# Nine pinned w2^T blocks with ScalarE casts, an input-gradient pass by tiles, and two orders, in a fused spectral and MLP layer with its gradients

## The chip, the cores and the metric

The kernel runs on one core of a Trainium2 chip. The metric is the device time of one execution in microseconds (us); the kernel before took 1411.57 us, the median of 3 runs (1410.99 to 1412.05). Besides the engines of the profile (PE is TensorE, DVE VectorE, ACT ScalarE, POOL GpSimd, SP SyncE) the kernel uses PSUM tiles of 128 x 512 in three groups: two buffers of "s", two of "d" and four of "f".

## What is computed

A layer with adaptive layer norms, a spectral mixer and a channel MLP, with its output and the gradients of all nine inputs by which it depends on parameters or data. x is 2048 x 1024, the MLP is 1024 to 3584 and back, all in bf16.

```python
def A(x, w_r, w_i):                       # spectral mixer
    X = rfft2(x) * (w_r + 1j * w_i)
    return irfft2(X, s=(2048, 1024))
def B(x, w1, b1, w2, b2):                 # MLP
    h = gelu(layernorm(x) @ w1 + b1)
    return h @ w2 + b2
def f(A_x, A_w_r, A_w_i, w1, b1, w2, b2, c, w_mod):
    sa, ca, ga, sb, cb, gb = split6(silu(c) @ w_mod)
    x = A_x
    x = x + ga * A(layernorm(x) * (1 + ca) + sa, A_w_r, A_w_i)
    return x + gb * B(layernorm(x) * (1 + cb) + sb, w1, b1, w2, b2)
out, vjp = jax.vjp(f, ...); return out, *vjp(grad_out)
```

## The kernel before

The transforms are done as matmuls on folded data: even and odd halves are formed by additions on DVE ("fold"), multiplied with cosine and sine matrices on PE, and taken apart again ("unfold"). The stages stand in this order, and the work of several lies beside each other, since the tile framework orders each engine's queue ahead of time by priorities and dependencies. Every engine takes its own queue in order.

**Front.** The modulation rows come from pm matmuls (mod_block, line 278, and its evacuation in line 281). At the same time the product of w2 with the transposed gradient, called ph, is begun: 28 blocks of 128 rows of w2^T, each of four PSUM tiles of 8 matmuls of 128x512 (ph_part, pp in line 814), so 32 matmuls for a block. A tile is cast to bf16 (line 820) into phs, a ring of four blocks in SBUF (three in pho, one in phr), and a block is stored on the POOL queue (line 822). Its w2 rows come by a transposing DMA on SP into wt, also a ring of four (load_w2t, line 341; block n can be loaded once block n-4 has been multiplied). PH_EARLY (line 824) says how many blocks are pinned: here 6 in a loop that also loads the blocks to come and puts the later pm groups behind blocks 3 and 5, and one more behind it (line 834). The last of these matmuls is early_pe, and the first matmuls of the forward spectral part may only be issued after it (line 537). The other blocks (line 897) are free: the scheduler puts them wherever PE has room within the spectral part and after it, and loads blocks from PH_EARLY + 4 on there.

**Forward fold.** For four chunks of x, the statistics (DVE and ACT), the norm (norm_act, line 514, four ACT instructions for a chunk), the modulation (line 194, the helper that records all tensor_tensor operations) and the fold fill fbuf. The last addition (fold_in) also releases the memset of css, a pair of staging buffers.

**Forward spectral part.** s_fwd multiplies fbuf with smA or smB (pu, lines 531 and 538; the forward pu use only the two "s" buffers) and copies to U, pcs (line 577), the filter pairs, pv (line 647), po (line 749), then consume_fwd: unfold, the residual, the second layer norm, and a store of the normed chunk. The copies of pu, pcs and pv are left to the framework's choice of engine (act_copy, line 778).

**MLP forward and the gradient at its inside.** z_block multiplies with w1 (pz, line 951) and evaluates the gelu and its derivative on ACT (lines 954 to 964) and DVE; z0 comes first, then the last blocks of ph, then z1 and on; pbo (line 1005) is the second MLP product.

**Input gradient, in quarters b of 512 rows.** pg_pass (line 1099) multiplies the gradient inside the MLP with w1^T: for each half h of the 1024 columns, four PSUM tiles i (128 rows each) and seven groups g of four matmuls, g outer and i inner, 28 steps of four matmuls. All four tiles are complete only in the last group. They are evacuated on ACT (line 1121, with their row sums). In quarters after the first, DVE and ACT run the layer-norm gradient (ln_bwd: lines 1199 to 1204, where ACT's line 1203 waits for two small DVE results), and fold the quarter into fbuf. The strip sums (acc3a, line 217) of the quarter before are put behind chosen steps of pg_pass by "behind". At the end the backward spectral part starts with pu (line 538) from this fbuf.

**Backward spectral part and w1's gradient.** The backward spectral part is interleaved by hand with products of the w2 and w1 gradients: fill(n) issues n pieces, where a piece of w1's gradient is one tile of 16 matmuls (gw1acc, line 1464, evacuated to gwo in line 1468). In consume_bwd (line 1376 on) a chunk i is followed by fill((4, 7, 6, 8)[i]), then a sum on PE over the product ct (halves_sum, accCA in line 217), then fill(2). After the spectral part the gradient of sa is scaled by ACT into sr (line 1521), whose buffer px0 was that of xt, the chunk of x that DVE reads in consume_bwd. Then the rest of w1's gradient fills PE to the end.

Of the kernel before, what the change touches and what calls it, by code (L numbers as in the profile page):

```python
# [10 lines left out]
FP32 = mybir.dt.float32  # L11
# [6 lines left out]
P = 128  # L18
S = 2048
D = 1024  # L20
# [3 lines left out]
NFC = F // P  # L24
KH = D // 2
# [5 lines left out]
NB = 4  # L31
# [4 lines left out]
def kernel(  # L36
# [24 lines left out]
    nc = tc.nc  # L61
# [4 lines left out]
    reg = ctx.enter_context(tc.tile_pool(name="reg", bufs=1))  # L66
# [6 lines left out]
    def ps_s(name):  # L73
        return psum.tile([P, 512], FP32, tag="s", name=name)
# [4 lines left out]
    def ps_f(name):  # L79
        return psum.tile([P, 512], FP32, tag="f", name=name, bufs=4)  # L80
# [44 lines left out]
    def chunk_rows(dt, i):  # L125
        return dt[4 * i * P:4 * (i + 1) * P, :].rearrange("(q p) d -> p q d", p=P)
# [14 lines left out]
    def load_tok(t4, src, i, eng=None):  # L141
        s3 = tok_flat(src)
        ins = (eng or nc.sync).dma_start(out=tok_plain(t4, i), in_=tok_rows(s3, i, 0, D))  # L143
        for q in range(2):
            nc.gpsimd.indirect_dma_start(out=t4[:, tok_idx(i, q), :], out_offset=None, in_=s3,  # L145
                                         in_offset=bass.IndirectOffsetOnAxis(ap=xidx[:, 2 * i + q:2 * i + q + 1], axis=0))
        return ins
# [45 lines left out]
    def tt(out, a, b, op):  # L193
        return nc.vector.tensor_tensor(out=out, in0=a, in1=b, op=op)  # L194
# [121 lines left out]
    def unfold_d(o4, tmp):  # L316
        n = o4.shape[1]
        ov = o4.rearrange("p c (a b w) -> p c a b w", b=2, w=256)
        tv = tmp.rearrange("p c (s b w) -> p c s b w", s=2, w=256)
        tt(tv[:, :, 0], ov[:, :, :, 0, :], ov[:, :, :, 1, :], ALU.add)  # L320
        tt(tv[:, :, 1], ov[:, :, :, 0, :], ov[:, :, :, 1, :], ALU.subtract)
        fwd = o4.rearrange("p c (b w) -> p c b w", w=512)[:, :, :, 0:256]
        rev = bass.AP(tensor=o4.tensor, offset=o4.offset + 1023, ap=[o4.ap[0], [D, n], [-512, 2], [-1, 256]])
        tt(fwd, tv[:, :, :, 0, :], tv[:, :, :, 1, :], ALU.add)
        tt(rev, tv[:, :, :, 0, :], tv[:, :, :, 1, :], ALU.subtract)

    def unfold_tok(o4, tmp):
        tt(tmp[:, 0:4:2, :], o4[:, 0:4:2, :], o4[:, 1:4:2, :], ALU.add)
        tt(tmp[:, 1:4:2, :], o4[:, 0:4:2, :], o4[:, 1:4:2, :], ALU.subtract)
        tt(o4[:, 0:4:3, :], tmp[:, 0:2, :], tmp[:, 2:4, :], ALU.add)  # L330
        tt(o4[:, 1:3, :], tmp[:, 0:2, :], tmp[:, 2:4, :], ALU.subtract)
# [8 lines left out]
    def load_w2t(fc):  # L340
        w2t_in[0] = nc.sync.dma_start_transpose(out=wt[:, fc % 4], in_=B_w2[fc * P:(fc + 1) * P, :])
        w2ts.append(w2t_in[0])
# [40 lines left out]
    for j in range(4):  # L383
        for cch in range(NDC):
            pt = ps_f("pt")
            for a in range(4):
                q = (0, 2, 3, 1)[a] if j % 2 == 0 else (1, 3, 2, 0)[a]
                nc.tensor.matmul(pt[:, q * P:(q + 1) * P], lhsT=gos[j][:, a, cch * P:(cch + 1) * P], rhs=(ident, irev)[a // 2],
                                 start=True, stop=True)
# [129 lines left out]
    def behind(ins, later):  # L519
        tc.add_manual_dep(ins.ins, later.ins.name, mybir.DependencyInfo(mybir.DependencyClass.NoSync, mybir.DependencyReason.DATA),  # L520
                          reason="order")
# [282 lines left out]
    last_pe = [None]  # L804
# [4 lines left out]
    def ph_part(fc, js):  # L809
        ph2 = phs[fc % 4]  # L810
        for j in js:
            pp = ps_f("pp")
            for cch in range(NDC):
                last_pe[0] = nc.tensor.matmul(pp[:], lhsT=wt[:, fc % 4, cch, :], rhs=gBoT[j][:, cch, :],  # L814
                                              start=(cch == 0), stop=(cch == NDC - 1))
            q = (0, 2, 3, 1)[j]
            ov = ph2[:, :, q * P:(q + 1) * P]
            pv = pp[:, :].rearrange("p (i w) -> p i w", w=P)
            with tc.high_priority():
                nc.any.tensor_copy(out=ov, in_=pv)  # L820
        if js[-1] == 3:
            nc.gpsimd.dma_start(out=d_ph[fc * P:(fc + 1) * P, :], in_=ph2.rearrange("p i w -> p (i w)"))

    PH_EARLY = 6
    late_mods = [(r, h) for r in (2, 3, 4) for h in range(2)]
    for fc in range(PH_EARLY):
        ph_part(fc, (0, 1, 2, 3))
        load_w2t(fc + 4)
        if fc in (3, 5):
            with tc.issue_after(last_pe[0].ins):  # L830
                for r, h in late_mods[3 * (fc // 2 - 1):3 * (fc // 2)]:
                    mod_block(r, h)

    ph_part(PH_EARLY, (0, 1, 2, 3))
    early_pe = last_pe[0]

    for i in range(4):
# [50 lines left out]
    def load_w1(n):  # L888
        for _ in range(n):
            g = len(w1s)  # L890
            wtile = reg.tile([P, NDC, BW], BF16, name=f"w1_{g}", tag=W1T[g])
            with tc.issue_after(w2t_in[0].ins):
                w1_in.append(nc.sync.dma_start(out=wtile[:], in_=w1_v[:, :, g * BW:(g + 1) * BW]))
            w1s.append(wtile)

    PH_KEEP = NFC - 4
    for fc in range(PH_EARLY + 1, NFC):
        if fc >= PH_EARLY + 4:
            load_w2t(fc)
            load_w1({24: 1, 25: 1, 27: 5}.get(fc, 0))  # L900
        ph_part(fc, (0, 1, 2, 3) if fc < PH_KEEP else (0, 1))
# [165 lines left out]
    w1Ts = []  # L1067
    gzr = [reg.tile([P, 2, 4, BW], BF16, name=f"gzr{k}", tag=f"t{k}") for k in range(4)]
    gzs, g_sums, gn3s = {}, {}, {}

    def gn3_of(b):
        if b % 2 not in gn3s:
            gn3s[b % 2] = reg.tile([P, 4, D], BF16, name=f"gn3{'ab'[b % 2]}", tag=("uv3", "wt")[b % 2])
        return gn3s[b % 2]
# [11 lines left out]
    for g in range(7):  # L1086
        wtile = reg.tile([P, 4, D], BF16, name=f"w1T_{g}", tag=W1T[g])
        for k in range(4):
            fc = g * 4 + k
# [6 lines left out]
    last_pg = [None]  # L1096
    sums_in = [[], [], []]

    def pg_pass(b, h, pool, before=lambda: ExitStack()):
        pgs = [pool(k)("pg") for k in range(4)]  # L1100
        for g in range(7):
            for i in range(4):
                for k in range(4):
                    with before():
                        last_pg[0] = nc.tensor.matmul(pgs[i][:], lhsT=gzs[b, g][:, k, i * P:(i + 1) * P],  # L1105
                                                      rhs=w1Ts[g][:, k, h * KH:(h + 1) * KH],
                                                      start=(g == 0 and k == 0), stop=(g == 6 and k == 3))
                    last_pe[0] = last_pg[0]
                g0 = 3 if b == NB - 1 else 2
                if b > 0 and h == 0 and (g, i) in ((g0, 0), (g0 + 1, 2), (g0 + 2, 2)):  # L1110
                    for ins in sums_in[g - g0]:
                        behind(ins, last_pg[0])
                    sums_in[g - g0].clear()
            for k in range(4 if b < 2 and h == 1 else 0):
                nc.scalar.activation(out=gzs[b, g][:, k, :], in_=gzs[b, g][:, k, :], func=ACT.Identity,
                                     accum_out=gb1_acc[:, g * 4 + k, b:b + 1])
            if g < 6:
                yield
        for i in range(4):
            with tc.high_priority():  # L1120
                nc.scalar.activation(out=gn3_of(b)[:, i, h * KH:(h + 1) * KH], in_=pgs[i][:], func=ACT.Identity,  # L1121
                                     accum_out=g_sums[b][:, h, i:i + 1])
        yield
# [248 lines left out]
    def consume_bwd(i, o4, tmp, tmp2, n1, eb):  # L1372
        if i == 0:
            accCA.append(ps_s("accCA"))
            nc.vector.tensor_copy(out=sacc, in_=eb[:, 0, :])
        elif i == 2:
            tt(sacc, sacc, eb[:, 0, :], ALU.add)
        unfold_d(o4, tmp)
        unfold_tok(o4, tmp)
        load_tok(n1, A_x, i, nc.gpsimd)  # L1380
        with tc.issue_after(last_po[0].ins):
            norm_act(n1, n1, 0, i)
        tt(tmp, o4, n1, ALU.mult)
        s1c = small.tile([P, 4], FP32, tag="s1c")
        for q in range(4):
            t = 4 * i + q
            nc.vector.tensor_tensor_reduce(out=o4[:, q, :], in0=o4[:, q, :], in1=opca_row, scale=1.0, scalar=0.0,  # L1387
                                           op0=ALU.mult, op1=ALU.add, accum_out=s1c[:, q:q + 1])
            ln_bwd(o4[:, q, :], s1c[:, q:q + 1], n1[:, q, :], stats[:, 0, 0, t:t + 1], o4[:, q, :], tmp2[:, q, :])
        nc.sync.dma_start(out=n1, in_=chunk_rows(d_gx1, i))  # L1390
        tt(o4, o4, n1, ALU.add)
        store_tok(out_1, o4, i)
        fill((4, 7, 6, 8)[i])
        halves_sum(accCA[0], tmp, i == 0, i == 3)
        fill(2)
        if i == 3:
            rows = small.tile([P, D], BF16, tag="gmrow", bufs=1)
            store_halves(accCA[0], rows[0:64, 0:KH], tmp, 1)
# [77 lines left out]
    def fill(n):  # L1476
        for _ in range(n):
            next(todo)
        done[0] += n
# [36 lines left out]

    accSA = [ps_d("accSA0"), ps_d("accSA1")]
    colsum(accSA, sacc, True, True)
    sr = reg.tile([P, 2, 1, D], FP32, name="sr", tag="px0")
    for h in range(2):  # L1520
        nc.scalar.mul(out=sr[0:1, 0, 0, h * KH:(h + 1) * KH], in_=accSA[h][0:1, :], mul=8.0)
    unfold_d(sr[0:1, 0], sr[0:1, 1])
# [48 lines left out]
```

## Time and profile before

| | |
|---|---|
| time, median of 3 runs | 1411.57 us (1410.99 to 1412.05) |
| time of the profiled execution | 1412.42 us |
| its span, first to last instruction | 1410.6 us |
| mean granted clock of PE | 0.992 |
| busy: PE, DVE, ACT, POOL | 1374.2, 1072.4, 739.2, 351.2 us |
| matmuls | 6963 |

Rows of a timeline give the start, the time that the group takes, engine, line, operation, output and inputs, shape and count; in brackets stands the idle time before it and what released it. A row of the waits gives engine, tile and line, the engine and the tile waited for, the total in us, how often, and the longest. Rows of windows give the stretch, its length, and for PE, PE's weight loads, DVE, ACT and POOL the busy time and the number of instructions; then the granted clock as a share of full speed, the DMA share and GB/s. "SPq" rows are SP's own queue issuing DMAs.

### The profile page before, as it was taken

Reading aid. Unit: us, or ns where it says so; the run is one execution under the profiler, and the core shown is the slowest. Engines: PE = TensorE matmul, PEld = TensorE weight load, DVE = VectorE, ACT = ScalarE, POOL = GpSimd, SP = SyncE. Lnnn points to the kernel's source line nnn. Section 1 sums busy time; section 2 is a strip of 40 time slices with the busy share of each in tenths; the row PEclk is TensorE's granted clock in tenths of the full one; section 3 lists DMA queues with packets and bytes.
Section 4 is the critical chain, followed back from the end, with each engine's and each line's share of the span. In section 5 each row is a group of like instructions: output and inputs, shape, how many; then the busy total and the mean of one; then the engine's idle time right before and its main releaser. Section 6 shows DMA issues by size and latency. Waiting matters only on the chain. (4 is left out here: it accounts for less than half of the span.)

```text
span 1410.6 us, 18696 instructions
## 1 busy us (share of the span) xinstructions
PE 1374.2 (97%) x6963; PEld 664.5 (47%) x6963; DVE 1072.4 (76%) x1507; ACT 739.2 (52%) x1059; POOL 351.2 (25%) x436
## 2 busy tenths in 40 slices
PE   5998999999999999999999999999999999999999
PEld 2545565444444444444444444444544565444444
DVE  5897889987978777887620688999498757979960
ACT  4774667667877765665314583243622444434311
POOL 5510623201112122112210010112345330322341
PEclk8899999999999999999999999999999999999999
DMA  9972666899787777696999499996689996897971
GB/s 330 301 234 57 176 165 200 265 283 350 256 258 242 229 242 249 189 287 224 298 271 232 138 237 321 259 259 209 197 265 288 261 253 173 218 250 189 286 270 38
DMA packets 361265, 333.22 MB, mean 236 GB/s; under 512 B 208026, under 2 KB 303152, under 8 KB 361046
## 3 DMA queue, kind: packets, MB, share of 16 engines
q1 hardware_dynamic: 319990, 206.01, 55.9%
q0 software_dynamic: 35424, 120.78, 24.5%
q10 hardware_dynamic: 5760, 5.25, 1.2%
q8 instruction: 54, 0.88, 0.3%
q14 instruction: 37, 0.30, 0.1%
HBM read 166.77 MB, written 115.92 MB: 200 GB/s over the span
## 5 line engine op out<-in xcount | busy, mean ns | idle before, releaser
L1105 PE MATMUL pg<-w1T,gzr 128*128 128x512 bf16 x896 | 196.0, 379 | 2.8 <-ACT gn3b L1121 2.8
L814 PE MATMUL pp<-gBoT,wt 128*128 128x512 bf16 x896 | 197.9, 380 | 0.8 <-DVE phr L820 0.4
L1464 PE MATMUL gw1acc<-gzh,n3n 128*128 128x512 bf16 x640 | 140.0, 379 | 0.2 <-DVE gwo L1468 0.2
L1105 PEld LDWEIGHTS <-gzr 128*128 128x128 bf16 x896 | 86.6, 98 | 111.1 <-issue 8.5
L1464 PEld LDWEIGHTS <-n3n 128*128 128x128 bf16 x896 | 87.3, 98 | 107.1 <-issue 3.3
L951 PEld LDWEIGHTS <-w 128*128 128x128 bf16 x896 | 87.2, 98 | 107.0 <-issue 2.5
L814 PEld LDWEIGHTS <-wt 128*128 128x128 bf16 x896 | 87.5, 98 | 104.0 <-issue 1.5
L951 PE MATMUL pz<-n3Tb,w 128*128 128x512 bf16 x448 | 99.2, 379 | 1.0 <-DVE w2sD L1027 1.0
L951 PE MATMUL pz<-n3Ta,w 128*128 128x512 bf16 x448 | 98.7, 379 | 0.0
L1005 PEld LDWEIGHTS <-hhA 128*128 128x128 bf16 x608 | 59.0, 98 | 73.1 <-issue 2.8
L1239 PE MATMUL gw2acc<-gB,hhsA 128*128 128x512 bf16 x416 | 92.2, 379 | 0.0
L954 ACT ACTIVATE gt<-pz,b_col 128x512 bf16<-128x512 f32 x112 | 72.8, 683 | 33.2 <-PE pz L951 33.0
L962 ACT ACTIVATE gt<-gt 128x2048 bf16<-128x2048 bf16 x28 | 53.5, 1911 | 64.8 <-DVE gt L194 64.8
L194 DVE TENSOR_TENSOR gt<-gt,gt 128x2048 bf16<-128x2048 bf16 x56 | 68.6, 1224 | 19.8 <-ACT gt L964 18.5
L194 DVE TENSOR_TENSOR ct<-ct 128x2048 bf16<-128x2048 bf16 x68 | 80.6, 1218 | 0.9
L1468 ACT CAST gwo<-gw1acc 128x512 bf16<-128x512 f32 x50 | 28.4, 581 | 89.3 <-PE gw1acc L1464 78.5
L1247 ACT CAST gwo<-gw2acc 128x512 bf16<-128x512 f32 x40 | 23.3, 584 | 93.6 <-PE gw2acc L1239 90.5
L1239 PEld LDWEIGHTS <-hhsA 128*128 128x128 bf16 x416 | 40.7, 98 | 47.4
L1470 POOL DMA_DIRECT2D out_dram<-gwo x53 | 29.2, 554 | 129.8 <-DVE gwo L1468 67.6
L1464 PE MATMUL gw1acc<-gzu,n3n 128*128 128x512 bf16 x256 | 55.6, 379 | 1.2 <-ACT gwo L1468 1.2
L958 ACT ACTIVATE gt<-gt 128x2048 bf16<-128x2048 bf16 x28 | 53.5, 1909 | 2.1 <-DVE hhC L194 1.3
L964 ACT ACTIVATE gt<-gt 128x2048 bf16<-128x2048 bf16 x28 | 53.4, 1907 | 0.4
(347 smaller groups left out, 2558.4 us busy)
## 6 DMA issues: line engine op xcount, KB each, us to landing
gzr<-d_gz SPq DMA_DIRECT2D x28, 512.0 KB
wblk<-in_w_mod_dram SPq DMA_DIRECT2D x12, 1024.0 KB
out_dram<-otl POOLq DMA_DIRECT2D x48, 256.0 KB, 4.9
d_ph<-pho POOLq DMA_DIRECT2D x21, 512.0 KB, 6.0
d_hh<-hhA POOLq DMA_DIRECT2D x19, 512.0 KB, 5.1
w<-in_B_w_dram SPq DMA_DIRECT2D x7, 1024.0 KB
hhC<-d_ph SPq DMA_DIRECT2D x14, 512.0 KB
w2sA<-d_ph SPq DMA_DIRECT2D x14, 512.0 KB
```

The costliest lines, as they stand in the source:

```text
L194: return nc.vector.tensor_tensor(out=out, in0=a, in1=b, op=op)
L814: last_pe[0] = nc.tensor.matmul(pp[:], lhsT=wt[:, fc % 4, cch, :], rhs=gBoT[j][:, cch, :], start=(cch == 0), stop=(cch == NDC - 1))
L951: last_pe[0] = nc.tensor.matmul(pz[:], lhsT=w1s[g][:, cch, k * P:(k + 1) * P], rhs=n3T[:, cch, :], start=(cch == 0), stop=(cch == NDC - 1))
L954: z_in = nc.scalar.activation(out=zb[:, k, :], in_=pz[:], func=ACT.Identity, bias=b1_col[:, fc:fc + 1], scale=1.0)
L958: nc.scalar.activation(out=av, in_=zb, func=ACT.Square)
L962: nc.scalar.activation(out=sg, in_=bv, func=ACT.Sigmoid, scale=2.0 * GK)
L964: nc.scalar.activation(out=bv, in_=bv, func=ACT.Sigmoid, scale=-2.0 * GK)
L1005: last_pe[0] = nc.tensor.matmul(pbs[i][:], lhsT=hh[:, k, i * P:(i + 1) * P], rhs=wp[:, k, :], start=False, stop=(g == 6 and k == 3))
L1105: last_pg[0] = nc.tensor.matmul(pgs[i][:], lhsT=gzs[b, g][:, k, i * P:(i + 1) * P], rhs=w1Ts[g][:, k, h * KH:(h + 1) * KH], start=(g == 0 ...
L1239: nc.tensor.matmul(acc[:], lhsT=hh_of(fc)[:, t, :], rhs=gBs[t // 4][:, t % 4, h * KH:(h + 1) * KH], start=(t == 0), stop=(t == NT - 1))
L1464: nc.tensor.matmul(acc[:], lhsT=n3ns[t // 4][:, t % 4, cch * P:(cch + 1) * P], rhs=gz2[t // 8][:, t % 8, :], start=(t == 0), stop=(t == NT ...
L1470: eng.dma_start(out=out_4[cch * P:(cch + 1) * P, fg * 512:(fg + 1) * 512], in_=ob)
```

## The change

1. PH_EARLY is 9, the separate block behind the loop is gone. So 9 blocks (0 to 8) are pinned ahead of the forward spectral part where 7 were (0 to 6). The pinned loop now loads the blocks up to 12, before up to 9.
2. The casts of blocks 3 to 8 are put on ScalarE; before, the framework chose the engine for each.
3. pg_pass, for the first half of the columns in quarters after the first, goes through the groups in blocks (0, 1), (2), (3), (4, 5, 6), and within a block tile by tile, so that tile 0 is complete at step 19 of 28 (counted from 1), tile 1 at 22, tile 2 at 25 and tile 3 at 28. The strip sums are put behind the same numbers of steps as before.
4. In consume_bwd, chunk i = 2, seven pieces stand ahead of the sum and one behind it (before six and two).
5. sr gets the buffer smb.

```diff
-                nc.any.tensor_copy(out=ov, in_=pv)
+                (nc.scalar.copy if 3 <= fc < PH_EARLY else nc.any.tensor_copy)(out=ov, in_=pv)
...
-    PH_EARLY = 6
+    PH_EARLY = 9
...
-    ph_part(PH_EARLY, (0, 1, 2, 3))
     early_pe = last_pe[0]
...
-    for fc in range(PH_EARLY + 1, NFC):
+    for fc in range(PH_EARLY, NFC):
...
     def pg_pass(b, h, pool, before=lambda: ExitStack()):
         pgs = [pool(k)("pg") for k in range(4)]
-        for g in range(7):
-            for i in range(4):
-                for k in range(4):
-                    with before():
...
+        blocks = ((0, 1), (2,), (3,), (4, 5, 6)) if b > 0 and h == 0 else tuple((g,) for g in range(7))
+        steps = [(g, i, i == 3 and g == block[-1] and block) for block in blocks for i in range(4) for g in block]
+        for n, (g, i, ends) in enumerate(steps):
+            for k in range(4):
+                with before():
...
+            n0 = 12 if b == NB - 1 else 8
+            if b > 0 and h == 0 and n - n0 in (0, 6, 10):
+                at = (n - n0 + 2) // 5
+                for ins in sums_in[at]:
+                    behind(ins, last_pg[0])
+                sums_in[at].clear()
...
-        fill((4, 7, 6, 8)[i])
+        fill((4, 7, 7, 8)[i])
         halves_sum(accCA[0], tmp, i == 0, i == 3)
-        fill(2)
+        fill(1 if i == 2 else 2)
...
-    sr = reg.tile([P, 2, 1, D], FP32, name="sr", tag="px0")
+    sr = reg.tile([P, 2, 1, D], FP32, name="sr", tag="smb")
```

More of the change, by code (lines that the diff above doesn't have):

```diff
@@ L1100, in pg_pass @@
         pgs = [pool(k)("pg") for k in range(4)]
-        for g in range(7):
-            for i in range(4):
-                for k in range(4):
-                    with before():
[L1105 to L1114, printed above, removed]
+        blocks = ((0, 1), (2,), (3,), (4, 5, 6)) if b > 0 and h == 0 else tuple((g,) for g in range(7))
[3 more added lines that the diff above has]
+                with before():
+                    last_pg[0] = nc.tensor.matmul(pgs[i][:], lhsT=gzs[b, g][:, k, i * P:(i + 1) * P],
+                                                  rhs=w1Ts[g][:, k, h * KH:(h + 1) * KH],
+                                                  start=(g == 0 and k == 0), stop=(g == 6 and k == 3))
+                last_pe[0] = last_pg[0]
+            n0 = 12 if b == NB - 1 else 8
[4 more added lines that the diff above has]
+                sums_in[at].clear()
+            if not ends:
+                continue
+            for g, k in [(g, k) for g in ends for k in range(4 if b < 2 and h == 1 else 0)]:
                 nc.scalar.activation(out=gzs[b, g][:, k, :], in_=gzs[b, g][:, k, :], func=ACT.Identity,
                                      accum_out=gb1_acc[:, g * 4 + k, b:b + 1])
-            if g < 6:
+            if ends[-1] < 6:
                 yield
```

## Prediction

> **What bounds the kernel now.** First the page's first part, then the waits of PE.
>
> ```profile
> PE 1374.2 (97%) x6963; PEld 664.5 (47%) x6963; DVE 1072.4 (76%) x1507; ACT 739.2 (52%) x1059; POOL 351.2 (25%) x436
> ```
>
> ```profile
> PE pu L538 <- DVE fbuf L194: 5.1, 1, 5.1
> PE pg L1105 <- ACT gn3b L1121: 2.8, 1, 2.8
> ```
>
> PE is busy for 1374.2 us of a span of 1410.6: the bound, with 36.4 us of idle time in all. The change leaves the count of matmuls as it is, so it can win only idle time of PE and time in which PE runs slowly, and must lose by adding such time. The waits view puts names to the idle time; the change aims at the two rows above and at two smaller ones (accCA and gw1acc, below). The profiled execution took 1412.42 us, 1.8 more than its span, and lies 0.85 above the median of 1411.57. I work in its times and take 0.85 off at the end.
>
> Next the timeline of PE, of DVE and of ACT around the first of these waits, and the windows for the granted clock.
>
> ```profile
> 106.88 0.38 PE L538 MATMUL pu<-smA,fbuf 128*128 128x256 bf16 x2
> 107.10 9.66 PE L814 MATMUL pp<-gBoT,wt 128*128 128x512 bf16 x44
> 121.87 1.46 PE L538 MATMUL pu<-smA,fbuf 128*128 128x256 bf16 x6 [5.11 <-DVE fbuf L194]
> ```
>
> ```profile
> 122.00:124.00 2.00, 2.00 (x9) 1.08 (x8) 1.77 (x1) 1.17 (x2) 0.00 (x0) 0.50 0.00 0
> 124.00:127.00 3.00, 3.00 (x16) 2.13 (x15) 0.00 (x0) 1.17 (x2) 0.00 (x0) 0.50 0.01 3
> 127.00:128.00 1.00, 1.00 (x7) 0.74 (x6) 0.00 (x0) 0.58 (x1) 0.00 (x0) 0.57 0.00 0
> 128.00:132.00 4.00, 3.96 (x35) 3.15 (x33) 2.12 (x3) 3.12 (x6) 0.00 (x0) 1.00 0.00 0
> ```
>
> PE ends block 6 of w2^T at 106.9, issues two pu that fill the PSUM buffers, runs 44 pp matmuls (0.2195 us each) and stands for 5.11 us until the forward fold is written. Then it pays a second time: columns PE (with its matmuls) and PEclk show 9 + 16 + 7 = 32 matmuls in 6 us at a clock of 0.50 to 0.57. In the next 4 us it does 35, so 32 would take 3.7 us: **2.3 us lost to the clock**.
>
> **Parts 1 and 2: nine blocks pinned, blocks 3 to 8 cast on ScalarE.** Who ends the fold?
>
> ```profile
> 73.80 0.68 DVE L820 CAST phr<-pp 128x512 bf16<-128x512 f32 x1
> ...
> 77.17 2.29 DVE L194 TENSOR_TENSOR fbuf<-fbuf,rows 128x4096 bf16<-128x4096 bf16 x1 [0.98 <-ACT fbuf L514]
> ...
> 91.94 0.69 DVE L820 CAST pho<-pp 128x512 bf16<-128x512 f32 x1
> ...
> 101.75 2.35 DVE L194 TENSOR_TENSOR x<-fbuf 128x2048 bf16<-128x2048 bf16 x2
> ...
> 106.69 2.28 DVE L194 TENSOR_TENSOR fbuf<-fbuf,rows 128x4096 bf16<-128x4096 bf16 x1
> ...
> 121.12 0.69 DVE L194 TENSOR_TENSOR fbuf<-fbuf,sb_saf 128x1024 bf16<-128x1024 bf16 x1
> 122.19 1.77 DVE L857 MEMSET cs<- 128x2056 uint32 x1 [0.38 <-issue]
> ```
>
> ```profile
> 92.87 1.53 ACT L820 CAST pho<-pp 128x512 bf16<-128x512 f32 x3
> ...
> 98.94 3.51 ACT L514 ACTIVATE fbuf<-x,stats 128x1024 bf16<-128x1024 bf16 x3 [3.36 <-DVE stats L194]
> ```
>
> DVE runs without a gap from 77.17 to the fold's end at 121.81. The five casts of blocks 3 to 5 that it does between 73.80 and 91.94 go to ACT, 0.6 us each from start to start, 3.0 in all. I expect the fold to gain nothing from this, because ACT takes the place of DVE. By the order of the changed kernel, the three casts now on ACT amid the four norm instructions of x_1 make these end near 78.1, not 77.1: DVE starts 1.0 later. And the stats of x_3 now stand behind the x_2 fold on DVE (behind the 101.75 row, so at 102.1 when the casts and the later start are counted), so the four L514 of x_3, 1.17 each from the 3.51 for three, run from 102.2 to 106.8. DVE waits for them at the place of the 106.69 row. The fold ends at 121.9. Bounds: 118.8, if ACT were never late (3.0 earlier, and then PE is what ends last), and 124.3, if all five casts (0.48 each on ACT, from 1.53 for three less the last one's tail) fell ahead of the last norm. I take 121.9, nearest to the rows.
>
> PE: 64 pp matmuls (two blocks) after 106.9 take 14.05 us and end at 120.9 to 121.3, so the wait shrinks from 5.11 us to about 0.8, with 20 pp more done and two pu less: 4.2 us. Idle for 0.8 the clock should stay, another 2.3. In sentences that the rest doesn't need: the Trainium skill, "TensorE: Matmul & The Clock Gate", Part 1, puts the fall to half rate after an idle window of about 3.4 us, and the return after about 3.4 us of sustained work. By its figures the second price would be an estimated 1.7 us (half of 3.4); the rows show 6 us near half rate, and the sum goes by them.
>
> What is new behind it: the fold's end is followed on DVE by the memset of css (1.77 us), and in the changed order the copies of the first U chunks that fall to DVE stand behind it. So the first of two pu buffers is free at about 124.6 and PE stands about 1.4 us (bounds 0 and 2.4: no copy needed, or a whole memset and a copy). Up to the po matmuls the changed order also holds 4 more pp and 2 more pu (1.1 us). So 2.3 − 1.4 − 1.1 = −0.2: po starts where it started before, with 24 pp matmuls (5.3 us) already done. **At the first z, PE is 5.1 us early.**
>
> SP is passed too: the transpose for block 12 joins those for 10 and 11 and waits for block 8.
>
> ```profile
> 107.07 8.36 SPq L341 DMA_TRANSPOSE wt<-in_B_w_dram  x2
> 134.65 6.12 SPq L686 DMA_TRANSPOSE smi<-d_SF  x4
> ```
>
> It holds SP until some 122.5; what follows is issued at 134.65, so it costs nothing, nor do the stores of blocks 7 and 8 on POOL, whose next work needs the spectral pairs. Without that cover it would be 0 to 3 us.
>
> Is the lead kept?
>
> ```profile
> 323.03 7.07 PE L951 MATMUL pz<-n3Ta,w 128*128 128x512 bf16 x32
> ```
>
> ```profile
> 357.02 1.91 ACT L962 ACTIVATE gt<-gt 128x2048 bf16<-128x2048 bf16 x1 [1.51 <-DVE gt L194]
> 358.84 0.67 ACT L954 ACTIVATE gt<-pz,b_col 128x512 bf16<-128x512 f32 x1
> ```
>
> ```profile
> 837.00:992.00 155.00, 151.96 (x736) 66.70 (x735) 143.43 (x198) 58.48 (x88) 21.59 (x24) 1.00 0.92 251
> ...
> 222.00:323.00 101.00, 100.60 (x468) 45.66 (x467) 95.11 (x139) 63.80 (x95) 22.25 (x26) 1.00 0.87 266
> ```
>
> From 222 to 323 DVE is busy for 95.11 of 101 us with the consume part, which starts with po and so isn't early. PE comes to z0 at 317.9. ACT's second sigmoid (357.02) waits for DVE, and PSUM evacuations (358.84) are queued behind it, with z3 behind those. One or two casts fewer on DVE in this stretch make the sigmoid 1.2 us earlier, while PE is 5.1 earlier with about 1.5 to 2 of slack: PE gives back 0 to 2.5 us. I take 2.0, as DVE is nearly full. Front: **3.1 us** (bounds 0 and 6.5).
>
> **Part 3: the pg pass tile by tile.**
>
> ```profile
> 909.24 6.22 PE L1105 MATMUL pg<-w1T,gzr 128*128 128x512 bf16 x28
> 918.30 22.61 PE L1105 MATMUL pg<-w1T,gzr 128*128 128x512 bf16 x104 [2.84 <-ACT gn3b L1121]
> ...
> 997.80 2.46 PE L538 MATMUL pu<-smf,fbuf 128*128 128x256 bf16 x21
> ```
>
> ```profile
> 910.04 1.24 ACT L1203 ACTIVATE got<-n2u,sc 128x1024 bf16<-128x1024 bf16 x1 [7.72 <-DVE sc L1202]
> ...
> 916.43 1.24 ACT L1203 ACTIVATE got<-n2u,sc 128x1024 bf16<-128x1024 bf16 x1 [3.76 <-DVE sc L1202]
> 917.58 0.58 ACT L1121 ACTIVATE gn3b<-pg 128x512 bf16<-128x512 f32 x1
> ```
>
> ```profile
> 990.48 2.48 DVE L194 TENSOR_TENSOR fbuf<-fbuf,gzr 128x2048 bf16<-128x2048 bf16 x2
> ```
>
> In the last quarter the pass h=1 needs the PSUM of h=0, whose evacuations stand on ACT behind three L1203 that wait for DVE (to 917.67). In the changed order tile 0 is complete 6 steps (24 matmuls, 5.2 us) earlier, and its evacuation stands on ACT behind the first L1203: done near 912, the second behind the next L1203 near 913. PE then meets no wait: **−2.84**. What is late next: DVE writes the backward fold at 992.96 and PE reads it at 997.80, a slack of 4.84; 2.84 of it goes, 2.0 is left. The sums that DVE makes in this part are released at the same counts of steps as before, so no work of DVE is later. Bounds: −2.84 and 0.
>
> **Part 4: one product ahead of the sum.**
>
> ```profile
> 1267.07 0.61 PE L217 MATMUL accCA<-ct,ones_bf 128*32 128x512 bf16 x8 [1.59 <-DVE ct L194]
> ...
> 1276.28 3.62 PE L1464 MATMUL gw1acc<-gzh,n3n 128*128 128x512 bf16 x16
> ```
>
> accCA waits for ct. A product of 16 matmuls (3.46 at pitch) ahead of it covers 1.59 with 1.87 to spare: **−1.59**. The product comes from the later fill, so nothing is added; its evacuation is 16 matmuls earlier on an ACT and DVE with room. Bounds −1.59 and 0.
>
> **Part 5: the tag of sr.**
>
> ```profile
> 1323.43 2.29 DVE L194 TENSOR_TENSOR ct<-ct,xt 128x4096 bf16<-128x4096 bf16 x1 [2.50 <-DMA xt<-d_gx]
> ```
>
> ```profile
> 1325.89 1.06 ACT L1521 ACTIVATE sr<-accSA 1x512 f32<-1x512 f32 x2 [8.90 <-DVE ct L194]
> 1326.86 1.99 ACT L1468 CAST gwo<-gw1acc 128x512 bf16<-128x512 f32 x4
> ```
>
> ```profile
> 1327.47 51.96 PE L1464 MATMUL gw1acc<-gzu,n3n 128*128 128x512 bf16 x240 [1.20 <-ACT gwo L1468]
> ```
>
> sr lies in the buffer of xt, so ACT stands until DVE has read xt, and four gwo casts are queued behind it. In smb nothing is read so late; ACT had been idle for 8.9 us, so sr and the casts come early: **−1.20** (bounds −1.20 and 0). PE then runs to the end with no wait, so every us that arrives there is kept.
>
> **Sum.** 3.1 + 2.84 + 1.59 + 1.20 = 8.7; 1412.42 − 8.7 = 1403.7 for such an execution, and 1402.9 for the median.
>
> **Rivals.**
> - The front's gain is all given back at z (chance 0.20): DVE, full from 222 on, sets the time and PE waits for it. For it: 95.11 of 101. Against it: the casts taken off DVE, and z's first evacuations, which don't need the consume part. Gain 5.6: 1405.9.
> - The pg wait moves to 997.80 (0.12): DVE, busy for 143.43 of 155 us here, sets each quarter, and the reordered evacuations on ACT cost the fold over 2.0 us. Against it: the slack above. Gain 5.9: 1405.7.
> - The cover is missed (0.10): the fold ends late enough that the clock falls again. In the backward pg stage 2.84 us of idle left it at 1.00, 5.11 didn't: so a fold after some 124 to 126. Then of 5.1 is left about 5.1 − 2.5 − 2.3 = 0.3, and z and the smaller stalls take some of the rest: gain 2.5 to 5, 1406.6 to 1409.1.
> - Slower (0.06): ACT, which takes its queue in order, becomes the bound of the fold. All 24 casts of blocks 3 to 8 at 0.48 us are 11.5; if they, or their waits for PE, stand ahead of the norm of x_3, the fold ends at 133.4. This decides from a fold 8.4 us late (5.1 + 5.6 − 2.3): at 11.5 it is 1411.6 + 3.1 = 1414.7. Against it: 12 of the 24 come after that norm in the changed order, and 11 were on ACT before.
>
> **How the numbers follow.** The forecast has 0.52. The range reaches from the front kept whole (gain 12.1: 1399.5) to the missed cover (1409.1) and a little beyond for the terms that may give 0: 1399 to 1410. A measurement of this kernel tells 0.2%, or 2.8 us, from no change. Faster by more: 0.80 (forecast, most of the first two rivals); within: 0.14 (the missed cover, and rests of the others); slower: 0.06.
>
> **What would show it.** In the profile of the changed kernel: the wait pu L538 under 1.5 us and the clock at 1.00 in 122 to 128; the fold's end between 121 and 123; a new wait of pu for U near 123; z0 near 318 and waits of pz between 340 and 365 of up to 2.5 us; no pg wait on gn3b; no accCA and no gw1acc wait of over 0.5. The forecast is wrong if the fold ends after 124, if pz waits for over 4 us, or if pu of the backward part (line 538) waits for fbuf.

## The result, and the profile after

The changed kernel takes 1422.16 us (median of 6 runs, 1420.86 to 1430.08), the kernel before 1411.81 in the runs beside it: a ratio of 1.0087, 95% interval 1.0065 to 1.0108. **It is 10.4 us slower by the medians (12.3 by the ratio), where 8.7 us faster was forecast**, and outside the range. Ratios here and below compare undisturbed executions alone, so they need not be the quotient of the medians. The profiled execution has a span of 1420.5 us, 9.9 more than before.

First the waits of PE in the changed kernel (columns: engine, tile and line, what it waited for, total us, times, longest).

```profile
PE pp L814 <- ACT pho L820: 5.8, 2, 5.6
PE pp L814 <- DMA wt<-in_B_w_dram: 4.7, 1, 4.7
PE pg L1105 <- DMA gzr<-d_gz: 3.7, 3, 1.8
PE pz L950 <- DVE w2sD L1026: 2.4, 1, 2.4
PE pu L538 <- DVE fbuf L194: 0.6, 1, 0.6
```

The waits that the change aimed at are gone: pu's has 0.6 us of its 5.1, pg's for gn3b (2.8), accCA's (1.6) and gw1acc's for ACT (1.2) are missing. In their place stand three large ones, 3.7 to 5.8 us each, the first two of them between 222 and 332 us; before, casts cost pp 0.8 us, and no load of w2^T and no gzr was waited for. PE's timeline shows the place, of the kernel before first and then of the changed one.

```profile
222.32 91.68 PE L814 MATMUL pp<-gBoT,wt 128*128 128x512 bf16 x424
314.40 8.79 PE L814 MATMUL pp<-gBoT,wt 128*128 128x512 bf16 x40 [0.40 <-DVE phr L820]
```

```profile
222.01 84.77 PE L814 MATMUL pp<-gBoT,wt 128*128 128x512 bf16 x392
311.52 7.04 PE L814 MATMUL pp<-gBoT,wt 128*128 128x512 bf16 x24 [4.74 <-DMA wt<-in_B_w_dram]
324.14 7.70 PE L814 MATMUL pp<-gBoT,wt 128*128 128x512 bf16 x24 [5.58 <-ACT pho L820]
331.68 7.07 PE L950 MATMUL pz<-n3Ta,w 128*128 128x512 bf16 x32
```

po ends where it did (222.0), and 440 matmuls are left before z0 instead of 464: the 24 that the prediction counted as a lead of 5.3 us. Then PE stands twice, 10.3 us in all, and runs at half clock in between and behind (windows of the changed kernel; column PEclk is the third from the end):

```profile
312.00:318.00 6.00, 6.00 (x22) 2.42 (x21) 6.00 (x6) 0.00 (x0) 0.00 (x0) 0.73 1.10 297
...
324.00:328.00 4.00, 3.86 (x10) 1.25 (x10) 4.00 (x8) 2.23 (x3) 0.00 (x0) 0.50 1.02 325
```

The two groups of 24 matmuls in those stretches take 7.04 and 7.70 us, where 24 take 5.34 elsewhere in the kernel. z0 comes at 331.68, 8.65 us later than before (323.03), where 317.9 was forecast. The ledger of PE's time at marks of the two timelines, later than before in us:

| mark (before) | later by | what came in between |
|---|---|---|
| end of po (222.3) | -0.3 | front as forecast, 24 matmuls of lead |
| z0 (323.0) | +8.65 | 10.3 us of waits, some 4 us of slow clock, less the lead |
| first pbo (365.1) | +9.7 | pz for ACT 1.2, less 0.35 |
| pq, end of the MLP stage (747.5) | +10.9 | w2sD 2.4, before 1.0 |
| pg of the last quarter (909.2) | +14.9 | gzr 3.7, and small ones |
| acc3b in it (940.8) | +11.9 | 2.84 of gn3b gone |
| po behind the third chunk's sum (1274.5) | +10.75 | 1.59 of accCA gone, 0.5 of small waits |
| last 128 gw1acc (1379.3) | +9.8 | 1.20 gone, gwo 0.3 more |

So parts 3 to 5 won their waits almost to the digit. The time went in two places: 14 us against the forecast between po and z0, and 3.7 in pg.

**Where the first went** shows on DVE and on SP. DVE, with idle time in brackets, before and then after:

```profile
297.20 2.29 DVE L194 TENSOR_TENSOR ct<-ct,rows 128x4096 bf16<-128x4096 bf16 x1 [2.90 <-ACT ct L514]
299.41 1.22 DVE L194 TENSOR_TENSOR ct<-ct 128x2048 bf16<-128x2048 bf16 x1
```

```profile
309.18 1.22 DVE L194 TENSOR_TENSOR ct<-ct 128x2048 bf16<-128x2048 bf16 x1 [15.80 <-DMA d_n<-ct]
```

Before, DVE stood there for 2.90 us, and for ACT. Now it stands for 15.8 us, because the buffer that it wants to write is still to be read by the store of a normed chunk (d_n). That store is issued from SP. SP's queue before, then after (rows: start, how long the issue holds the queue):

```profile
283.10 4.87 SPq L936 DMA_TRANSPOSE n3Ta<-d_n  x1
288.13 1.23 SPq L341 DMA_TRANSPOSE wt<-in_B_w_dram  x1
291.92 0.39 SPq L879 DMA_DIRECT2D d_n<-ct  x1
...
295.04 3.21 SPq L341 DMA_TRANSPOSE wt<-in_B_w_dram  x1
```

```profile
277.07 16.20 SPq L935 DMA_TRANSPOSE n3Ta<-d_n  x1
293.36 3.10 SPq L341 DMA_TRANSPOSE wt<-in_B_w_dram  x1
296.63 0.46 SPq L892 DMA_DIRECT2D w<-in_B_w_dram  x1
297.18 3.23 SPq L878 DMA_DIRECT2D d_n<-ct  x1
300.50 4.22 SPq L341 DMA_TRANSPOSE wt<-in_B_w_dram  x1
```

The transposing load of n3Ta (z0's input) starts 6.03 us earlier and holds SP for 16.2 us instead of 4.87. Everything behind it is late: the load of block 24, the d_n store (297.2 for 291.9, and slower to land, so that DVE is free only at 309.2), and the load of block 25 of w2^T (300.5 for 295.0), for which PE stands 4.74. The second wait of PE, for a cast on ACT, is DVE's again. ACT's timeline has the cast behind a square root that waited 17.64 us for DVE's statistics:

```profile
323.32 0.30 ACT L479 ACTIVATE mv<-mv,eps_c 128x4 f32<-128x4 f32 x1 [17.64 <-DVE mv L490]
323.53 0.57 ACT L820 CAST pho<-pp 128x512 bf16<-128x512 f32 x1
```

**Why earlier?** In z_block that load is queued behind the load of block 23 (`with tc.issue_after(w2ts[23].ins) if b == 0`), and a load waits for its slot in the ring of four, that is, for PE to finish block 19. PE is 24 matmuls ahead, so the whole chain of loads is 5 to 6 us ahead, and n3Ta with it. The consume part, which starts with po, isn't.

**Where the second went:** quarter 2 and the last one (b = 2 and 3) of pg. First PE in the changed kernel, which had no such wait before, then SP in quarter 2, before and after.

```profile
864.27 1.04 PE L1105 MATMUL pg<-w1T,gzr 128*128 128x512 bf16 x4 [1.82 <-DMA gzr<-d_gz]
...
918.10 1.04 PE L1105 MATMUL pg<-w1T,gzr 128*128 128x512 bf16 x4 [1.59 <-DMA gzr<-d_gz]
```

```profile
836.01 6.59 SPq L1275 DMA_TRANSPOSE hb<-d_hh  x1
842.71 1.92 SPq L1081 DMA_DIRECT2D gzr<-d_gz  x3
```

```profile
841.20 13.53 SPq L1278 DMA_TRANSPOSE hb<-d_hh  x2
855.17 1.48 SPq L1080 DMA_DIRECT2D gzr<-d_gz  x3
```

With the last block (4, 5, 6) gone through tile by tile, group 6 is needed at step 19 of 28 and no longer at 25: 5.2 us sooner. Its load stands on SP behind two transposes that hold it for 13.5 us (the first row before is the second of the same two). The row of its load starts at 855.2, 12.5 us later than before, when PE is 10.9 us later: SP is only 1.6 us further behind PE, against the 5.2 us by which the order asks for the load sooner.

### The profile page after: what moved, and what is told of

The parts are those of the page before. It is cut to its first block, busy times and chain, and to the rows that moved or that the text cites. A ratio compares the mean times of both kernels' runs of the same rounds, so it can differ in the third digit from the quotient of the medians.

```text
span 1420.5 us, 18694 instructions
## 1 busy us (share of the span) xinstructions
PE 1375.7 (97%) x6963; PEld 663.0 (47%) x6963; DVE 1070.7 (75%) x1503; ACT 741.1 (52%) x1063; POOL 352.0 (25%) x436
## 5 line engine op out<-in xcount | busy, mean ns | idle before, releaser
L814 PE MATMUL pp<-gBoT,wt 128*128 128x512 bf16 x896 | 202.0, 384 | 10.6 <-ACT pho L820 5.8
L194 DVE TENSOR_TENSOR ct<-ct 128x2048 bf16<-128x2048 bf16 x68 | 80.6, 1216 | 16.8 <-DMA d_n<-ct 15.8
L1250 ACT CAST gwo<-gw2acc 128x512 bf16<-128x512 f32 x40 | 23.3, 585 | 93.6 <-PE gw2acc L1242 87.6
```

## The experiments

Two theories for the front. **SP queue:** the early transpose meets other transfers, holds SP, and what stands behind it stops DVE and PE. **Lead:** DVE and ACT can't follow a PE that is 5 us ahead, whatever SP does. The kernel before ran beside each run.

| run | median us | ratio to before | 95% interval |
|---|---|---|---|
| e1_front | 1427.99 | 1.0110 | 1.0081 to 1.0140 |
| e2_rest | 1408.27 | 0.9977 | 0.9963 to 0.9991 |
| e3_n3_late | 1409.49 | 0.9985 | 0.9972 to 0.9998 |
| e4_dn_act | 1412.62 | 1.0002 | 0.9981 to 1.0024 |
| e5_before_n3_early | 1417.45 | 1.0025 | 1.0001 to 1.0049 |
| e6_parts45 | 1410.42 | 0.9986 | 0.9976 to 0.9997 |
| e7_rest_pg3 | 1407.67 | 0.9966 | 0.9953 to 0.9980 |
| e8_n3_late_pg3 | 1412.23 | 0.9997 | 0.9983 to 1.0010 |
| e9_dx_later | 1410.72 | 0.9996 | 0.9979 to 1.0013 |
| e10_pin8 | 1408.25 | 0.9970 | 0.9957 to 0.9983 |
| e11_no_act_casts | 1410.68 | 0.9988 | 0.9970 to 1.0005 |
| e12_all_mended | 1410.48 | 0.9999 | 0.9985 to 1.0012 |

**e1_front: parts 1 and 2 alone** (the hunks of lines 820 to 897 applied to the kernel before).

> Parts 1 and 2 alone. In the changed kernel PE comes to the first z 8.65 us later than before (331.68 against 323.03) and loses 1.0 more by the first pbo and 1.3 in front of pa's group. Theory 'front loses, rest gains': this kernel shows the whole loss, first z near 331 to 332, and lacks the gains of parts 3 to 5 (5.6 us). If the waits of pg for gzr (3.7 us) belong to part 3, they are absent here and the time is about 1424 (1411.8 + 8.65 + 1.0 + 1.3, and 0.6 to 1.5 of small things). Rival 'gzr waits come with the late front': they are here, and the time is about 1427. The pair of both says whether the transpose of n3Ta holds SP for 16 us again (theory) or whether that was one execution's accident (rival: 5 us, and first z near 318).

Measured 1427.99. The transpose holds SP for 12.18 us, DVE stands 23.3 us for the d_n store, PE 8.9 for loads of w2^T and 8.3 for a cast; z0 comes at 338.6, later still than forecast, so that the time is the one that the rival gave, though its waits didn't come. No wait for gzr stands among its large ones: those belong to part 3. The long hold is no accident of one execution.

**e2_rest: parts 3 to 5 alone** (those hunks undone in the changed kernel).

> Parts 3, 4 and 5 without 1 and 2. Theory 'part 3 calls for the last groups of gz up to 5 us sooner and so meets their DMAs': gains of 2.84, 1.59 and 1.20 less pg waits for gzr of up to 3.7, so 1406.2 to 1410. Rival 'the gzr waits come with the late front': no such wait, 1406.2. No loss ahead of 760 us in either.

1408.27, a gain of 0.23% where 5.6 us (0.40%) of waits were removed. gzr waits of 1.8 us are there without any change in the front: they come with the tile order.

**e3_n3_late: the changed kernel with the transpose behind a later load.**

```diff
-            with tc.issue_after(w2ts[23].ins) if b == 0 else ExitStack():
+            with tc.issue_after(w2ts[25].ins) if b == 0 else ExitStack():
```

> The changed kernel, with the transposing load of n3Ta put behind the load of block 25 of w2^T instead of block 23; on SP the second store of d_n then stands ahead of it. Theory 'SP queue': the 16.2 us that the transpose holds SP delay the d_n store (DVE waits 15.8 us for its buffer) and the load of block 25 (PE waits 4.7); with the order turned both go, first z at 318 to 322 and time 1408 to 1413. Rival 'DVE and ACT can't keep up with PE's lead': DVE still stands at the same place or PE waits for evacuations, first z at 328 or later, time 1418 to 1423.

```profile
291.98 0.39 SPq L878 DMA_DIRECT2D d_n<-ct  x1
292.46 2.02 SPq L341 DMA_TRANSPOSE wt<-in_B_w_dram  x1
294.58 7.13 SPq L935 DMA_TRANSPOSE n3Ta<-d_n  x1
301.89 1.08 SPq L892 DMA_DIRECT2D w<-in_B_w_dram  x2
```

(SP's queue.) The store is out at 292.0, the transpose holds SP for 7.1 us, DVE stands 4.4 instead of 15.8, and z0 comes at 322.1. **1409.49: one number in one line takes back 12.7 us of 1422.16 by the medians**, as the SP theory had it. But z0 is only 0.9 us ahead of the kernel before, not 5.1, since a load of w2^T is now late behind the transpose (PE waits 2.9 and then takes 8.77 us for 32 matmuls instead of 7.07).

**e4_dn_act: the stores of d_n from ACT's queue.**

```diff
-        nc.sync.dma_start(out=chunk_rows(d_n3, i), in_=tmp)
+        nc.scalar.dma_start(out=chunk_rows(d_n3, i), in_=tmp)
```

> The changed kernel, with the stores of d_n issued from ACT's queue instead of SP's. Theory 'SP queue': DVE's wait of 15.8 us for the store goes or falls below 5, as the store no longer stands behind the transpose; the wait of PE for the load of block 25 (4.7 us) may stay, since that stands behind the transpose still: first z at 320 to 327, time 1411 to 1418. Rival 'the transfers themselves are slow (all 16 DMA engines taken)': the store still lands late, DVE stands 10 us or more, time 1419 to 1423.

In the profiled execution (1406.38) the transpose still holds SP, 277.86 to 291.34, yet DVE stands 4.3 us and z0 comes at 320.58: the harm of the hold is what is queued behind it. PE doesn't wait for the load of block 25 either, as it was thought it might. The kernel as a whole is erratic, though: 1405.1 to 1420.2 in the ten runs behind its ratio, with a median in the expected 1411 to 1418. The profile is of one of the shortest; what made the others longer is open.

**e5_before_n3_early: the kernel before, with the transpose one block earlier.**

```diff
-            with tc.issue_after(w2ts[23].ins) if b == 0 else ExitStack():
+            with tc.issue_after(w2ts[22].ins) if b == 0 else ExitStack():
```

> The kernel before with one thing changed: the transposing load of n3Ta is put behind the load of block 22 of w2^T, not 23, so that it starts near 276 (in the changed kernel 277.07, before 283.10) while everything else is as before. Theory 'the start near 277 is what makes the transpose hold SP for 12 to 16 us, whatever PE does': SP is held for over 10 us here too, and DVE or PE waits behind it; time up by 2 to 10, 1414 to 1422, the less as the d_n store and the loads need SP a little later here. Rival 'it needs the lead of PE': the transpose takes 5 to 7 us, time 1410 to 1413.

```profile
275.55 15.97 SPq L936 DMA_TRANSPOSE n3Ta<-d_n  x1
291.61 10.93 SPq L341 DMA_TRANSPOSE wt<-in_B_w_dram  x2
302.63 0.53 SPq L879 DMA_DIRECT2D d_n<-ct  x1
```

With nothing of the change in it, the hold is 15.97 us, DVE stands 12.8 for the store, PE 5.0 for w2^T and 4.8 for a cast, z0 comes at 335.0, and the profiled execution takes 1426.24. The ten runs behind the ratio reach from 1409.62 to 1428.44, and by the ratio e5 is 0.25% slower than the kernel before, where e1 is 1.10% slower. That the meeting is struck in some and missed in others is the likely reading, but the short ones left no profile. So the start near 276 can do the harm without PE's lead; in the changed kernel it is the lead that brings this start about.

**e9_dx_later: what does the transpose meet?** In the changed kernel the 1 MB store of d_x of the third chunk starts at 277.42, in the middle of it; before, at 277.74, 5.4 us ahead of it. Here that store goes behind the chunk's norm on ACT (issued at 295.24).

```diff
-        nc.gpsimd.dma_start(out=chunk_rows(d_x1, i), in_=x4)
+        if i != 2:
+            nc.gpsimd.dma_start(out=chunk_rows(d_x1, i), in_=x4)
...
         norm_act(tmp, x4, 1, i)
+        if i == 2:
+            with tc.issue_after(norm_in[0][-1].ins):
+                nc.scalar.dma_start(out=chunk_rows(d_x1, i), in_=x4)
```

> The changed kernel; the store of d_x of the third chunk (1 MB, issued at 277.42 in the changed kernel, 0.3 us behind the start of the n3Ta transpose) is issued from ACT's queue behind the norm of that chunk instead, near 297. Theory 'the transpose holds SP for 16 us because it meets that store in the DMA engines (in the kernel before the store had left 5.4 us ahead of it)': the hold falls to 5 to 8 us and the time to 1408 to 1414. Rival 'it is slow with or without that store': hold 12 to 16 us, time 1416 to 1424.

SP's queue, and then the windows (last columns: clock, DMA share, GB/s) of this kernel and of the changed one over the same stretch.

```profile
279.30 4.54 SPq L939 DMA_TRANSPOSE n3Ta<-d_n  x1
284.87 1.23 SPq L341 DMA_TRANSPOSE wt<-in_B_w_dram  x1
```

```profile
286.00:290.00 4.00, 4.00 (x20) 1.83 (x19) 4.00 (x13) 3.50 (x7) 0.10 (x1) 1.00 1.12 216
290.00:296.00 6.00, 6.00 (x30) 2.74 (x28) 2.80 (x7) 5.56 (x7) 0.96 (x2) 1.00 0.74 265
```

```profile
286.00:290.00 4.00, 4.00 (x20) 1.75 (x19) 3.02 (x9) 3.49 (x5) 0.54 (x1) 1.00 1.29 165
290.00:296.00 6.00, 6.00 (x29) 2.74 (x28) 1.54 (x4) 5.56 (x7) 0.53 (x1) 1.00 1.29 76
```

The hold is 4.54 us, though the transpose still starts 3.8 us earlier than in the kernel before (in e12, with the same edit, 4.46 us from 277.70), and the time is back at 1410.72. In the changed kernel the engines show as full (1.29) while they move 76 GB/s; here they move 265. So the partner of the collision is that store: with it within 1.3 us of the transpose's start the hold was 12.2 to 16.2 us (the changed kernel, e1, e4, e5), without it 4.5. Why a store of 1 MB, which landed in 4.9 us before, keeps a transposing load some 11 us longer is open. It isn't the only thing that can: in e11 the hold was 10.0 us, 20 us behind that store, and that wasn't followed up.

**e6_parts45 and e7_rest_pg3: what is part 3 worth?** e6 has parts 4 and 5 alone; e7 has parts 3 to 5 with the tile order in the last quarter alone:

```diff
-        blocks = ((0, 1), (2,), (3,), (4, 5, 6)) if b > 0 and h == 0 else tuple((g,) for g in range(7))
+        blocks = ((0, 1), (2,), (3,), (4, 5, 6)) if b == NB - 1 and h == 0 else tuple((g,) for g in range(7))
```

> Parts 4 and 5 alone. Both theories: waits of accCA (1.59) and of gw1acc on ACT (1.20) gone, 1409.2 less whatever. Beside the run of parts 3 to 5 (1408.3) this says what part 3 is worth by itself: theory 'its 2.84 us are partly paid back by waits for gzr (1.8)': the two times differ by about 1; rival 'paid back in whole': no difference.

> Parts 3, 4 and 5, but the tile order of part 3 only in the last quarter, where PE had waited 2.84 us for gn3b. Theory 'the tile order costs by calling for late gz groups sooner in quarters that had no wait to lose': the gzr wait of quarter 2 goes, that of quarter 3 stays, time 1 below the run of parts 3 to 5: 1407. Rival 'the waits come from chance in the DMA': equal to it, 1408.3.

1410.42 and 1407.67: ratios of 0.9986 and 0.9966. Against e2 (0.9977) part 3 as written is worth some 0.1%, and in the last quarter alone some 0.2%, where its 2.84 us are; e7 has 0.6 us of gzr waits left. The intervals overlap, so the order of the three is likely and not shown. **e7 has the lowest time measured**, 0.34% below the kernel before, and 14.5 us below the changed one by the medians; e10 below can't be told from it.

**e8, e10, e11, e12: is the lead of the front worth anything, once SP is in order?** e8 is e3 with e7's tile order. e10 is e7 with 8 blocks pinned (PH_EARLY = 7 in the kernel's old form) and the transpose behind block 24. e11 is e3 with all casts left to the framework. e12 is e9 with e7's tile order, so all five parts with both repairs.

> The changed kernel with n3Ta behind block 25's load and with the tile order in the last quarter alone: whether both repairs together beat the kernel before and the run of parts 3 to 5 alone (1408.3). If the lead of the front can be kept once SP is in a better order, 1404 to 1407; if the front gives nothing, as in the run with n3Ta late (first z at 322), 1407 to 1409.

> Parts 3 (last quarter alone), 4 and 5, with 8 blocks pinned (before 7, changed 9), their casts left to the framework, and n3Ta behind block 24's load, so that it starts near 288. Theory 'a lead of PE is worth nothing at z, since DVE and ACT set the pace there': within 0.2% of the same kernel with 7 blocks (1407.7), the wait for fbuf near 2 and waits of pz and w2sD larger by as much. Rival 'with SP in order the lead is kept': 1404 to 1406.

> The changed kernel with n3Ta behind block 25's load, as in the run with n3Ta late (1409.5), and the casts of blocks 3 to 8 left to the framework (part 2 undone). Theory 'the casts on ACT move the fold's end by nothing (121.7 in the changed kernel, 121.8 before)': fold's end 121 to 123, the same time within 2 us. Rival 'they are what lets nine blocks fit': the fold ends at 124 or later, DVE doing some of the casts of blocks 6 to 8 as well, and the time rises by 2 to 4.

> All five parts, with the d_x store of the third chunk moved as in the run before last (1410.7) and the tile order of part 3 in the last quarter alone. Against parts 3 to 5 without the front (1407.7, ratio 0.9966): theory 'the front's lead of 5 us is handed back behind z (waits of pz, pbo and casts), so it is worth nothing even with SP free': ratio 0.996 to 0.999, 1407 to 1411. Rival 'the lead is kept once SP is free': ratio 0.993 to 0.995, 1402 to 1405.

Measured 1412.23, 1408.25, 1410.68 and 1410.48. None is faster than e7, which has none of the front's change. e8 lies above what was expected of it, with waits of pz for ACT and for w2sD of 3.5 us each. e11 has the fold's end at 121.24 with no cast put on ACT, and e3's time within the intervals: no effect of part 2 is seen. (Its profiled execution, 1414.9, is one of its longest: PE waits 10.4 us for a load of w2^T behind the transpose, and z0 comes at 328.69.) e12 has z0 at 319.59, 3.4 us ahead of the kernel before, and loses it again; PE's timeline and its windows:

```profile
359.88 1.89 PE L954 MATMUL pz<-n3Ta,w 128*128 128x512 bf16 x8 [0.45 <-ACT gt L957]
362.25 1.89 PE L954 MATMUL pz<-n3Ta,w 128*128 128x512 bf16 x8 [0.49 <-ACT gt L957]
...
445.52 3.42 PE L954 MATMUL pz<-n3Tb,w 128*128 128x512 bf16 x8 [2.38 <-DVE w2sD L1030]
```

```profile
446.00:450.00 4.00, 4.00 (x12) 1.42 (x11) 3.90 (x4) 2.28 (x5) 1.41 (x1) 0.61 0.95 267
```

At the first pbo 1.0 of the lead is left (364.07 for 365.08); the w2sD wait is 2.38 where it was 1.04, and the 8 matmuls behind it run at half clock (3.42 us for 1.89): at pq PE is 2.1 us later than before (749.60 for 747.54). So the lead of 5 us ends as a loss in this execution. The ratios agree: 0.9999 for e12 against 0.9966 for e7, with intervals that lie apart, though e12 differs from e7 by the moved store as well as by the front. In this the lead theory had a point: with SP in order, waits for DVE and ACT eat the lead. Why the w2sD wait is longer in the changed kernel, e1, e3, e9 and e12 (2.4 us; 3.5 in e8) than in e2, e5, e6, e7 and e10 (1.1; 0.9 in e11) wasn't followed up.

## Why the prediction was wrong, point by point

- **The front itself came as worked out.** Fold's end 121.6 (forecast 121.9), wait for fbuf 0.61 (0.8), clock 1.00 from 120 to 128, a new wait for the U copy of 1.32 (1.4), po in place (222.0), 24 matmuls of lead.
- **The step that failed** is "SP is passed too [...] It holds SP until some 122.5; what follows is issued at 134.65, so it costs nothing". For that stretch it held: the three transposes hold SP to 122.2, and what follows is issued at 133.77. But the step followed the one load that the change moves across the fold, and stopped there. Each later load is released by PE's progress too, so the lead moved every one of them by 5 to 6 us against the consume part, and with them the load that the code chains to block 23. Its place in the queue was unchanged; its time wasn't: 277.07 for 283.10, a hold of 16.2 us for 4.87, and z0 at 331.68 where 317.9 was forecast. e5 shows that this shift alone can do the harm in the kernel before, and e9 and e12 that one store makes it.
- "Front: 3.1 us (bounds 0 and 6.5)" had no bound below nothing, because the stalls were sought at z alone, where the rows of before showed slack. The place of the loss, 300 to 324 us, was passed as "SP, costs nothing".
- The first rival (all given back at z, 0.20) is close to what is left when SP is mended: e10 is as fast as e7. In e12 more than the gain goes, by waits for ACT and for w2sD and by the clock.
- "The slower rival" had the right sign at 0.06, and the wrong mechanism: ACT's casts moved the fold by nothing.
- **Part 3:** the 2.84 us went, and the fold's slack held (fold written at 1004.5, pu at 1009.7). "Bounds: -2.84 and 0" left out that a tile order reads the last groups 5.2 us sooner; the loads' row wasn't looked at, and 3.7 us of waits came.
- **Parts 4 and 5:** both waits gone; together 0.14% by e6 (interval 0.03 to 0.24%), 0.20% forecast.
- The slow clock was rightly taken as a second price, and at 122 it wasn't paid. It was paid behind the two waits ahead of z0 instead, and its condition and size aren't as the prediction took them (below).

## What to carry to other kernels

When a change makes the bounding engine run ahead, list every DMA whose issue that engine's progress releases, and every DMA chained behind those by order, and lay their new times beside the transfers that don't move: the queue's order can stay as it was while its meetings change. A queue that issues in order turns one slow issue into the lateness of whatever stands behind it, so look for the store that frees a buffer there. And when a loop order is changed to finish one output sooner, check that its inputs are there as much sooner.

## What the runs showed of the hardware that wasn't expected

The transposing load held its issuing queue for 4.5 to 7.8 us in e2, e3, e6 to e10 and e12 (10.0 in e11), where it ran clear of the 1 MB store, and for 12.2 to 16.2 us in the changed kernel, e1, e4 and e5, the engines showing as full at 76 GB/s towards its end in the changed kernel.

The clock can fall after shorter idle times than the prediction took from 2.84 (kept) and 5.11 (lost). In e10 PE stood for 2.97 us ahead of 120.41 and then had half clock:

```profile
120.00:122.00 2.00, 1.59 (x11) 1.09 (x12) 1.62 (x2) 1.06 (x2) 0.00 (x0) 0.88 0.00 0
122.00:124.00 2.00, 2.00 (x11) 1.40 (x10) 0.50 (x1) 1.12 (x3) 0.00 (x0) 0.50 0.02 4
124.00:126.00 2.00, 2.00 (x15) 1.40 (x14) 0.43 (x1) 1.24 (x3) 0.00 (x0) 0.77 0.00 0
```

In e12 2.38 us of idle were enough, while 2.84 in the kernel before weren't, nor was the same wait for w2sD, of 2.4 us too, in the changed kernel, e1, e3 and e9, where the clock stayed at 1.00. The Trainium skill, "TensorE: Matmul & The Clock Gate", Part 1, has the fall after an idle window of about 3.4 us, in a window that runs freely. These runs show falls at 2.38 and 2.97 us, so idle time below that figure isn't safe here.

Where the clock is either full or half, a mean clock c over 2 us means 4(1 - c) us at half rate, so the slow stretch in e10 lasted about 0.5 + 2.0 + 0.9 = 3.4 us. That is also the Trainium skill's figure for the return (same page, Part 1). By the same working it was 3.4 us in e7 too, and 6.8 us, twice that, in the kernel before (windows from 120 to 128: 0.76, 0.50, 0.50 and 0.53), where the prediction counted the 6 us behind the wait. The length of the wait didn't set which: 5.1 us of wait gave 6.8 us in the kernel before and 3.4 in e5.
